# Key, query and tile-partial stores on the SyncE queue, first backward tiles pipelined, fewer warm-up matmuls

## The chip, the cores and the metric

One core of one Trainium2 chip. The metric is the device time of one execution in microseconds (us), lower is better. Where a time stands alone it is the median of the runs of one kernel on one chip.

## The reference

Forward and gradients of a block `x + s * g`. `g` is a gated MLP. `s` is attention over 64 segments of 32 tokens, each of which first sees 8 memory rows that the segment before it produced:

```python
H, Dh = (32, 128)               # 32 heads of 128; Dm = 640, S = 2048
M, seg = (8, 32)                # 8 memory rows, segments of 32 tokens
mem = mem0
for s in range(n_seg):          # 64 segments, one after another
    xs = x[:, s * seg_len:(s + 1) * seg_len, :]
    h = jnp.concatenate([mem, xs], axis=1)
    q, k, v = (einsum('btd,dhe->bhte', h, W) for W in (Wq, Wk, Wv))   # shortened
    scores = jnp.where(mask, einsum('bhqe,bhke->bhqk', q, k) * scale, -1e9)
    p = softmax(scores)
    o = einsum('bhte,hed->btd', einsum('bhqk,bhke->bhqe', p, v), Wo)
    mem = o[:, :M, :]
    outs.append(o[:, M:, :])
...
_out, _vjp = jax.vjp(_f, A_x, A_mem0, A_Wq, A_Wk, A_Wv, A_Wo, B_w1, B_w3, B_w2)
_grads = _vjp(grad_out)
```

The 64 memory updates are a serial chain, forward and again backward. The change touches those two chains and the start of the second.

## The kernel before

One forward step (`chain`) projects 32 columns with each weight: the 8 memory rows of this segment, and 24 *later* tokens that ride along. Keys, queries and values of these 32 rows are staged in a tile of 128 partitions by 1024 and stored. Three staging tiles a step share two buffers:

```python
WARM = dict(G1=1, G2=2, G3=3, G4=4, G5=3, G6=2)
...
def stage():
    return ch.tile([P, 1024], BF16, name="stg", tag="stg", bufs=2)

def dump(sg, dst, q=nc.gpsimd):
    q.dma_start(dst.rearrange("r (g c) -> g r c", g=4), sg[:])
sk = stage()
half(Wk_, 0, sk, 'v')
half(Wk_, 1, sk, 'v')
...
sq = stage()
...
dump(sk, k.KS[t])
...
sv = stage()                                # waits for the store of sk
packed_half(k, bA, hx, Wv, 0)
...
k.copy(sv[:, 0:512], bA[:], eng='s')        # line 92 of a helper, ACT
dump(sq, k.QVS[t, :, 0])
...
nc.scalar.copy(sTm[:], psT.rearrange("p a q h -> p a (q h)"))     # scores, ACT too
...
dump(sv, k.QVS[t, :, 1], nc.sync)
```

`gap("G2")` and the like, left out above, are places between the links of the chain into which other work is put (attention for the tokens, in tiles of 96), and then `WARM` matmuls whose result nobody reads; they keep TensorE's clock up:

```python
def gap(g):
    FILL(g, t, at, kbatch)
    ...
    for i in range(WARM.get(g, 0)):
        nc.tensor.matmul(bB[:], k.ident[:], Wq[:, 0, 0:512], start=True, stop=True)
```

Keys, queries and values of the first 672 tokens (`NB0`) were computed ahead and lie in order. Those of later tokens lie where the steps put them, in rows 8 to 32 of each step's block, so that 96 tokens are a block of 4 by 24 rows. The gradient rows (`g_src`) are likewise in order only from token 1344 (`GB0`) on:

```python
if x0 + nx <= self.NB0:
    return [(0, nx, X0[x0:x0 + nx])]                        # 96 rows in order
...
if r == 0 and nx - a >= 48:
    nt = (nx - a) // 24
    out.append((a, a + 24 * nt, XS[t:t + nt, 8:32]))        # 4 x 24 rows
...
def g_src(self, tl, c0, c1):
    ...
    return [(0, 96, self.GOS[8 + 4 * tl:12 + 4 * tl, 8:32, c0:c1])]   # 4 x 24 rows
```

The backward chain, cut to what the change touches:

```python
WARM = dict(G1=2, G2=3, G5=3, G6=2)
...
def load_xp(t):
    xp = ch.tile([P, 8, 2, 32], F32, name="xp", tag="xp", bufs=1)
    nc.sync.dma_start(xp[:], k.GXP[t // 3, :, :, t % 3])
...
sg = ch.tile([P, 1024], BF16, name="gstg", tag="gstg", bufs=1)
...
nc.sync.dma_start(k.GOS[t].rearrange("r (g c) -> g r c", g=4), sg[:])
...
def ld(tl, qd):                              # loads of a tile part, 4 ahead
    ...
    nc.sync.dma_start(qv[0:nm], k.m_src(tl, "qv", c0, c0 + 512))
    k.load_x(qv, nm, k.x_src(tl, "qv", c0, c0 + 512), nc.sync)
    k.load_x(gor, nm, k.g_src(tl, c0, c0 + 512), nc.sync)
    ...
def gmem(tl, qd):                            # tile partials, summed by gkv in a later step
    ...
    ks = fl.tile([P, ns, 2, 4, 8], F32, name="gks", tag="gks", bufs=1)
    ...
    nc.gpsimd.dma_start(k.GXP[tl, :, qd, 0:ns], ks[:].rearrange("p s i h m -> p s i (h m)"))
```

## Time and profile before

| | before |
|---|---|
| median of the runs before the prediction | 6971.42 us (3 runs, 6968.43 to 7006.38) |
| forward recurrence, 63 steps | 1613.1 us, 25.6 a step |
| start of the backward stage | 120.6 us |
| backward recurrence from its second step | 1482.0 us (2780.0 to 4262.0), 23.2 a step |

A step is the time from one step's first projection matmul to the next one's. The table can be checked against the page of the kernel before, of which these are the span and two rows of the slices (40 equal slices; granted clock in tenths of full, and busy share of the 16 DMA engines in tenths):

```profile
span 6956.7 us, 170429 instructions
...
PEclk9888888888888886888888997999999999885789
DMA  6473444444344554555555665233222233455673
```

The forward recurrence is slices 4 to 13, the backward one slices 16 to 25. The clock's digit is 8 in every slice of the first and 6 to 9 in the second; the means over the two stages are 0.87 and 0.88. The rest of the profile before is shown in the prediction.

### The profile page before, as it was taken

Reading aid. Unit: us, or ns where it says so; the run is one execution under the profiler, and the core shown is the slowest. Engines: PE = TensorE matmul, PEld = TensorE weight load, DVE = VectorE, ACT = ScalarE, POOL = GpSimd, SP = SyncE. Lnnn points to the kernel's source line nnn. Section 1 sums busy time; section 2 is a strip of 40 time slices with the busy share of each in tenths; the row PEclk is TensorE's granted clock in tenths of the full one; section 3 lists DMA queues with packets and bytes.
Section 4 is the critical chain, followed back from the end, with each engine's and each line's share of the span. In section 5 each row is a group of like instructions: output and inputs, shape, how many; then the busy total and the mean of one; then the engine's idle time right before and its main releaser. Section 6 shows DMA issues by size and latency. Waiting matters only on the chain. (4 is left out here: it accounts for less than half of the span.)

```text
span 6956.7 us, 170429 instructions
## 1 busy us (share of the span) xinstructions
PE 5767.0 (83%) x69516; PEld 3253.2 (47%) x69516; DVE 2419.9 (35%) x7541; ACT 1878.1 (27%) x5180; POOL 1184.8 (17%) x1811
## 2 busy tenths in 40 slices
PE   6777999898888775888888895988999988775688
PEld 3444444444444443555455553555555555342244
DVE  5433444444444212443334441222222222011752
ACT  3332444344334212222222221222222222000301
POOL 0001333333334102333333330000000000000000
PEclk9888888888888886888888997999999999885789
DMA  6473444444344554555555665233222233455673
GB/s 193 147 263 111 103 108 107 107 105 108 104 106 111 138 186 124 147 152 141 142 139 152 158 156 89 78 93 82 80 76 78 77 93 89 105 146 180 195 176 95
DMA packets 1039599, 876.70 MB, mean 126 GB/s; under 512 B 550536, under 2 KB 947304, under 8 KB 1029600
## 3 DMA queue, kind: packets, MB, share of 16 engines
q1 hardware_dynamic: 614330, 517.84, 27.3%
q10 hardware_dynamic: 337894, 213.14, 11.1%
q0 software_dynamic: 86592, 134.83, 7.9%
q8 instruction: 547, 8.96, 0.6%
q14 instruction: 236, 1.93, 0.1%
HBM read 556.09 MB, written 309.09 MB: 124 GB/s over the span
## 5 line engine op out<-in xcount | busy, mean ns | idle before, releaser
L1199 PE MATMUL g<-w,gT 128*128 128x512 bf16 x2112 | 622.7, 385 | 0.8 <-ACT gT L92 0.8
L1216 PE MATMUL wg<-gr,hr 120*128 120x512 bf16 (+1 forms) x2640 | 578.5, 379 | 1.0 <-DVE ghacc L1205 0.5
L1200 PE MATMUL g<-w,gT 128*128 128x128 bf16 x2112 | 466.9, 221 | 0.0
L662 PE MATMUL bank<-Wq,ident 128*128 128x512 bf16 x960 | 352.1, 474 | 138.1 <-ACT stg L92 138.1
L1216 PEld LDWEIGHTS <-hr 120*128 120x128 bf16 (+1 forms) x2640 | 254.0, 98 | 321.4 <-issue 22.6
L1199 PEld LDWEIGHTS <-gT 128*128 128x128 bf16 x2112 | 209.3, 99 | 220.9 <-issue 13.9
L1205 DVE TENSOR_TENSOR ghacc<-ghacc,g 120x512 f32<-120x512 f32 (+1 forms) x154 | 105.8, 687 | 563.4 <-PE g L1199 563.4
L1096 PE MATMUL gbank<-WqT,ident 128*128 128x512 bf16 x640 | 226.7, 461 | 83.6 <-DVE gkv L871 83.6
L1209 POOL CAST gxo<-ghacc 120x640 bf16<-120x640 f32 (+1 forms) x22 | 15.8, 720 | 1590.3 <-issue 1476.3
L92 ACT COPY gT<-t6g 128x480 bf16<-128x480 bf16 (+1 forms) x352 | 191.8, 545 | 331.1 <-PE t6g L1190 215.8
L337 PEld LDWEIGHTS <-gkv 128*8 128x8 bf16 x8192 | 201.7, 94 | 157.3 <-issue 49.8
L318 PEld LDWEIGHTS <-hx 128*32 128x32 bf16 x7680 | 178.0, 96 | 189.5 <-DVE xPT L624 25.5
L90 DVE CAST stg<-bank 128x512 bf16<-128x512 f32 x256 | 177.0, 691 | 235.9 <-PE bank L318 209.1
L604 ACT ACTIVATE xP<-xsp,xnm 120x120 bf16<-120x120 f32 (+1 forms) x704 | 239.7, 359 | 28.9 <-DVE xrz L614 18.2
L484 DVE COPY vt<-stg 8x512 bf16<-8x512 bf16 x512 | 144.5, 282 | 273.2 <-ACT stg L92 267.0
L90 DVE CAST wgo<-wg 128x512 bf16<-128x512 f32 x72 | 47.5, 688 | 543.6 <-PE wg L1216 499.0
L1241 PE MATMUL oa<-gow,orr 120*128 120x512 bf16 x704 | 197.2, 383 | 35.3 <-DMA orr<-OR 35.3
L1190 PE MATMUL t6g<-ident,gr 120*128 120x120 bf16 (+1 forms) x2112 | 187.9, 219 | 43.3 <-ACT gT L92 40.8
L983 POOL DMA_DIRECT2D VTD<-gvT x176 | 132.7, 789 | 462.9 <-ACT gvT L982 452.1
L1200 PEld LDWEIGHTS <-gT 128*128 128x128 bf16 x2112 | 209.0, 99 | 0.3
L615 POOL TENSOR_TENSOR xP<-xP,xrz 120x480 bf16<-120x480 bf16 (+1 forms) x176 | 170.3, 967 | 212.9 <-DVE xrz L614 202.9
L337 PE MATMUL gbank<-WvT,gkv 128*8 128x320 bf16 x4096 | 202.1, 366 | 0.0
(317 smaller groups left out, 11964.6 us busy)
## 6 DMA issues: line engine op xcount, KB each, us to landing
gqv<-QVS SPq DMA_DIRECT2D x112, 192.0 KB
vTt<-VTD SPq DMA_DIRECT2D x64, 320.0 KB
OR<-xv POOLq DMA_DIRECT2D x168, 120.0 KB, 4.6
VTD<-gvT POOLq DMA_DIRECT2D x168, 120.0 KB, 5.7
orr<-OR SPq DMA_DIRECT2D x8, 2520.0 KB
PR<-xP POOLq DMA_DIRECT2D x168, 112.5 KB, 7.0
gPr<-PR SPq DMA_DIRECT2D x168, 112.5 KB
DSR<-gdS POOLq DMA_DIRECT2D x168, 112.5 KB, 4.6
```

The lines of the kernel that those rows point to most:

```text
L90: return nc.vector.tensor_copy(out, in_)
L92: return nc.scalar.copy(out, in_)
L318: k.nc.tensor.matmul(bank[32 * g:32 * g + 32, :], x[:, dc, :], W[:, dc, c0:c0 + 512], start=(dc == 0), stop=(dc == k.DC - 1), tile_positio ...
L337: k.nc.tensor.matmul(pm[p0:p0 + nq, 0:320], x[:, h, :], W[:, h, 320 * b:320 * b + 320], start=(first and i == 0), stop=(last and i == 15), ...
L604: nc.scalar.activation(Pb[0:n, j, 0:n], sp[0:n, j, :], ACT.Exp, bias=nmx[0:n, j:j + 1], scale=k.scale, accum_out=Z[0:n, j:j + 1])
L662: nc.tensor.matmul(bB[:], k.ident[:], Wq[:, 0, 0:512], start=True, stop=True)
L1096: nc.tensor.matmul((bA if g[0] == "W" or g == "G1" else bB)[:], k.ident[:], WqT[:, 0, 0:512], start=True, stop=True)
L1190: nc.tensor.transpose(pt[:, j, :], gr[0:n, i, j * P:(j + 1) * P], k.ident[0:n, 0:n])
L1199: nc.tensor.matmul(g5[:], gT[:, i, j, :], W[:, j, 0:512], start=f, stop=l)
L1200: nc.tensor.matmul(g1[:], gT[:, i, j, :], W[:, j, 512:640], start=f, stop=l)
L1216: nc.tensor.matmul(accs[dc][:], hr[0:n, tl, dc * P:(dc + 1) * P], grs[tl][0:n, 2 - i, :], start=(tl == 0), stop=(tl == NTL - 1))
L1241: nc.tensor.matmul(ac[j][0][:], lh, gow[0:n, tl, 0:512], start=(tl == 0), stop=(tl == NTL - 1))
```

## The change

The intent: the value copy waits for the key store, so send that store earlier, from the SyncE queue; load the tile partials earlier; pipeline the 19 tile parts at the start of the backward stage; and drop warm-ups (15 to 7 a step forward, 10 to 4 backward), which should no longer be needed once the stalls are gone.

```diff
-            WARM = dict(G1=1, G2=2, G3=3, G4=4, G5=3, G6=2)
+            WARM = dict(G2=2, G3=1, G4=2, G5=2)
...
-                def dump(sg, dst, q=nc.gpsimd):
+                def dump(sg, dst, q=nc.sync):
...
-            WARM = dict(G1=2, G2=3, G5=3, G6=2)
+            WARM = dict(G1=1, G5=2, G6=1)
...
-                nc.gpsimd.dma_start(k.GXP[tl, :, qd, 0:ns], ks[:].rearrange("p s i h m -> p s i (h m)"))
+                nc.sync.dma_start(k.GXP[tl, :, qd, 0:ns], ks[:].rearrange("p s i h m -> p s i (h m)"))
...
-            for qd in range(8):
-                ld(k.NTL - 1, qd)
-                turn(k.NTL - 1, qd)
-                dprob(k.NTL - 1, qd)
-                dsoft(k.NTL - 1, qd)
-                gmem(k.NTL - 1, qd)
...
-            batch = {T - 1: [(k.NTL - 2, qd) for qd in range(8)] + parts[0]}
+            pro = [(tl, qd) for tl in (k.NTL - 1, k.NTL - 2) for qd in range(8)] + parts[0]
+            batch = {}
...
-                    if t == T - 1:          # (and the 11 parts that ran one after another in it)
...
                     elif g == "G4":
+                        if t > 0:
+                            load_xp(t - 1)
                         at(dsoft, t, 1)
...
                     elif g == "G6":
                         at(dsoft, t, 2)
-                        if t > 0:
-                            load_xp(t - 1)
...
+            todo = pro + todo
+            for _ in range(4):
+                ld_next()
+            for i in range(len(pro) + 2):
+                for f, o in ((turn, 0), (dprob, 1), (dsoft, 1), (gmem_ld, 2)):
+                    if 0 <= i - o < len(pro):
+                        f(*pro[i - o])
```

More of the change, by code (lines that the diff above doesn't have):

```diff
@@ L915, in chain @@
                 bd(nc.vector, bdS, dS)
-                if 0 < t < T - 1:
+                if t > 0:
                     loads(t - 1)
@@ L1061, in gap @@
                 def gap(g):
-                    if t == T - 1:
-                        if g == "G6":
-                            for u in batch[t]:
-                                ld_next()
-                                for f in (turn, dprob, dsoft, gmem):
-                                    f(*u)
-                            loads(t - 1)
-                            load_xp(t - 1)
-                            for _ in range(4):
-                                ld_next()
-                    elif g == "W0":
+                    if g == "W0":
                         at(turn, t, 0)
@@ L1075, in gap @@
                         at(turn, t, 1)
-                        if t + 1 < T - 1:
-                            at(gmem_ld, t + 1, 2)
+                        at(gmem_ld, t + 1, 2)
                     elif g == "G1":
@@ L1085, in gap @@
                     elif g == "G4":
+                        if t > 0:
+                            load_xp(t - 1)
                         at(dsoft, t, 1)
@@ L1092, in gap @@
                         at(dsoft, t, 2)
-                        if t > 0:
-                            load_xp(t - 1)
                     for i in range(WARM.get(g, 0)):
```

## The prediction

> **What bounds the kernel now.** I read the page's slices first, to see which stages the change touches and what clock they ran at; then the page's costliest groups, for the warm-up matmuls; then the waits of each engine, in the forward recurrence (611 to 2224 us of the span) and the backward one (2780 to 4242 us) separately; then the timeline of one step of each.
>
> The windows view of the forward recurrence, the start of the backward stage, and the rest of it:
>
> ```profile
> 610.90:2224.00 1613.10, 1445.58 (x22245) 767.10 (x22247) 701.51 (x2089) 626.70 (x2212) 585.30 (x787) 0.87 0.40 103
> 2659.40:2780.00 120.60, 57.31 (x782) 37.63 (x782) 37.44 (x249) 23.91 (x98) 35.42 (x62) 0.57 0.40 112
> 2780.00:4242.30 1462.30, 1247.01 (x24559) 772.28 (x24558) 590.42 (x2766) 376.52 (x1228) 484.74 (x840) 0.88 0.56 144
> ```
>
> The columns are length, busy PE, weight loads, DVE, ACT, POOL, then granted clock. The three stretches are 3196 of 6957 us; nothing else is touched. PE is busy 90% and 85% of the two recurrences, but not all of that is work. A forward step lasts 25.6 us, a backward one 23.2. The groups with the warm-up matmuls:
>
> ```profile
> L662 PE MATMUL bank<-Wq,ident 128*128 128x512 bf16 x960 | 352.1, 474 | 138.1 <-ACT stg L92 138.1
> L1096 PE MATMUL gbank<-WqT,ident 128*128 128x512 bf16 x640 | 226.7, 461 | 83.6 <-DVE gkv L871 83.6
> ```
>
> That is 15 warm-ups a step forward and 10 backward, and nearly the only real idleness of PE stands in front of them: 138.1/64 = 2.2 us a step forward, 83.6/64 = 1.3 us backward. Behind the first are ACT's waits in the forward stage:
>
> ```profile
> ACT stg L92 <- DMA KS<-stg: 306.3, 57, 12.4
> ACT stg L92 <- DMA OR<-xv: 28.9, 6, 5.6
> ```
>
> The staging tile has two buffers and three users a step (key, query, value), so the value copy waits until the key store has landed. One step's timeline, cut to this chain:
>
> ```profile
> 1406.20 0.76 POOL L456 DMA_DIRECT2D KS<-stg  x1
> ...
> 1413.80 1.07 ACT L92 CAST stg<-bank 128x512 bf16<-128x512 f32 x2 [5.23 <-DMA OR<-xv]
> ...
> 1414.93 0.58 PE L662 MATMUL bank<-Wq,ident 128*128 128x512 bf16 x1 [2.28 <-ACT stg L92]
> 1415.24 0.37 ACT L491 CAST sTm<-bank 40x256 bf16<-40x256 f32 x1
> ```
>
> The data for the value copy was ready at 1409.1; the copy began at 1413.8. ACT works in order, so the scores copy (L491), on which the recurrence hangs, is late too. The backward counterpart, in the waits of DVE, PE, ACT and POOL:
>
> ```profile
> DVE gkv L871 <- DMA xp<-GXP: 135.1, 28, 7.4
> PE gbank L1096 <- DVE gkv L871: 82.7, 62, 5.6
> PE gbank L326 <- ACT gstg L92: 49.0, 16, 5.6
> ACT gks L1027 <- DMA GXP<-gks: 164.4, 72, 9.0
> POOL gox L826 <- DMA gride<-GST: 78.9, 13, 8.4
> ```
>
> The load of the tile partials (xp) is issued at the end of a step and lands about 7.5 us later, after its user is ready. Every fourth step POOL waits for a token load; GXP stores queue behind that, ACT waits to reuse gks (one buffer), and the next step's gstg copy waits behind ACT.
>
> [...]the clock is half or full[...]: records are 0.5 or 1.0 and last multiples of 3.413 us. I summed the columns streamed in each window (512 columns at full clock are 0.21 us): in the forward stage the 63 windows after which the clock fell held 0.09 to 0.46 of a window's worth, and those after which it stayed full held at least 0.88; backward the two groups meet near 0.35. Each forward step falls once and stays cold 6.4 us on average.
> [...]Here the key store on GpSimd lands a median 7.0 us after issue; the value store, same shape, goes out on SyncE already and its last packet ends a median 7.4 us after issue. So the queue alone is not the gain. [...]This store is 4 by 32 by 1024; [...]about 23 of 2 KB in each half microsecond, 84 ns each, so four at a time, and 128 of them need 128 x 0.084 / 4 = 2.7 us at best.
>
> **The change part by part.**
> *Forward.* Mean marks of the 62 inner steps, from the first key matmul, us: value half ready 7.0; value copy 11.35; score matmuls end 9.6; scores transposed 13.1; softmax done 15.4; output product 17.6; Wo product 19.85 to 22.55; fold 23.65; next step 25.55. Now the key store goes out on SyncE as soon as the stage is filled, 3.2 us into the step (before: 4.1, behind an OR store). With 1.5 to 2 us to the first packet, 2.7 us of drain and about 1 us of sharing it should land near 9.0. Then the value copies end at 10.2, scores are transposed at 11.1 (-2.0), softmax is done at 13.2. Warm-ups in a row cost 0.22 us each at full clock (four in 1.04 us at 1395.71) and 0.42 at half (four in 1.89 us at 1421.78). Before the output product one is left of three, before Wo two of four: output product at 14.2, Wo at 15.8 to 18.2 (-4.0, half of it stall and half warm-ups and clock). The fold chain (ACT, DVE, ACT, DVE: 1.1 us) stays; dropping two warm-ups after it saves 0.3 us or so. Next step near 20.9: 4.6 us less. The stretch from 8.6 to 15.8 then holds 8048 columns, 3.35 us of 7.2, or 0.47: close to where the clock falls. I take off 0.6 us (40% of the steps cold, 1.5 us each): 4.0 x 63 = **252 us**.
> *Backward.* Steps without the xp stall and without a cold window exist: steps 24, 22, 17, 12 and 8 take 19.3 to 19.9 us with all ten warm-ups; in them the first output product starts at 8.0 us, in stalled ones at 11 to 15. The load now goes out in mid-step, right after its buffer's last reader, ahead of the tile loads; that is over 8 us earlier. GXP stores on SyncE no longer stand behind POOL's token wait. Three warm-ups between gkv and the product go, 3 x 0.22 = 0.65; the other three hide mostly behind the fold, 0.2. So 19.7 - 0.85 = 18.9, plus 0.9 for cold windows in most steps (unstalled steps with one take 20 to 21): 19.8 against 23.2, 3.4 x 62 = **211 us**.
> *Start.* From the first load (2659.4) to the second step (2780.0) are 120.6 us at clock 0.57: 8 tile parts in 37 us, then a first step of 83.8 that holds 11 more, one after another. Pipelined, 19 parts are limited by SyncE's issues, 2.6 to 2.9 us each plus 0.55 for the store, say 3.4: 65, plus 12 to fill and drain, plus a step of 21: 98. **22 us**.
> Sum 252 + 211 + 22 = 485; 6971 - 485 = 6486, so 6485.
>
> **The rivals.**
> *The store is no faster on SyncE.* For it: the 7.4 us of the value store. Against: that one has ten or so loads ahead of it in its ring, the key store two to four. The value copy would start at 10.6 instead of 9.0, costing 1.6 us a step, 100 us: 6585.
> *Fewer warm-ups, colder clock.* For it: 0.47 is near the 0.46 at which the clock has fallen. If both chains ran cold from scores to product in each step, forward would lose about 1 us more a step and backward as much: 125 us, 6610. Against: the stalls that caused the falls are what goes.
> *SyncE in order becomes the bound.* Its issues already take 15 to 20 us of a 25 us step in the middle of the backward stage, and gain 1.5; forward the loads now stand behind two stores that wait for data. If middle backward steps stick at 22 us, 90 us are lost: 6575. Against: SyncE waits 4.2 us a step for the krow buffer, and tile loads run four ahead.
> Two together give about 6700; all three about 6800, still over 2% less. To come within 2% (above 6832) the stalls must stay whole.
>
> **Range and chances.** One rival wholly or two in half give 6575 to 6630; everything going right (no cold windows) is near 6390. So 6390 to 6630, with faster 0.94, same 0.05, slower 0.01.
>
> **What would show it.** Right: forward step near 21.5 us and backward near 20; ACT's wait for the key store below 100 us in all (now 306); DVE's wait for xp gone; gstg waits under 15 us; clock above 0.92 in both stretches; start stretch near 98 us. Wrong: ACT still waiting for KS over 3 us a step (first rival); clock at or below 0.87 with short PE gaps (second); waits of PE or DVE for DMA loads of gqv, xq, xv or xp (third).

## The result

| | before | changed | predicted |
|---|---|---|---|
| median, same chip, 4 runs each | 6969.93 us | 6864.44 us | 6485 (6390 to 6630) |
| ratio (95% interval) | 1 | 0.984 (0.9805 to 0.9874) | about 0.93 |
| forward step, mean of all | 25.60 us | 24.69 us | 21.5 |
| of these steps 1 to 17 / 19 to 59 | 25.56 / 25.55 | **22.18 / 25.79** | no difference expected |
| backward step | 23.23 us | 22.46 us | 19.8 |
| start of the backward stage | 120.6 us | 126.0 us | 98 |

A ratio is the mean time of one kernel's runs over that of the other kernel's runs of the same rounds, so it is not quite the ratio of the medians quoted. The experiments ran on chips 7, 12 and 6; the times of the kernel before differ between chips by up to 0.4%, so they are compared with each other by ratio. Step times are from the profiled execution of each.

About 105 us were gained instead of 485. By stages of the two profiles: forward 1613.1 to 1555.6 (-57.5), backward 1482.0 to 1438.2 (-43.8), start +5.4. The sum, -95.9, is the difference of the spans, 6956.7 to 6863.8, within 3 us; nothing was lost elsewhere.

The windows view of the changed kernel, the same three stretches (length, busy PE, weight loads, DVE, ACT, POOL, granted clock, DMA share, GB/s):

```profile
612.30:2167.90 1555.60, 1305.35 (x21610) 730.35 (x21735) 709.10 (x2089) 625.15 (x2211) 487.92 (x659) 0.87 0.40 107
2603.10:2729.10 126.00, 46.02 (x774) 35.02 (x776) 37.42 (x250) 25.60 (x100) 24.66 (x43) 0.55 0.44 117
2729.10:4167.30 1438.20, 1166.57 (x24054) 769.96 (x24180) 589.81 (x2766) 381.38 (x1226) 396.74 (x683) 0.87 0.58 146
```

PE is busy 140 and 80 us less than before in the two recurrences, because the warm-ups are gone, but the stretches shrank by only 57 and 44: PE idles more. The clock is where it was. What PE waits for, in the waits of ACT and PE in the forward stretch (idle us, count, longest):

```profile
ACT stg L92 <- DMA KS<-stg: 309.7, 57, 8.7
PE bank L497 <- ACT sTm L491: 163.4, 63, 5.2
```

The wait of the value copy for the key store, 306.3 us before, is 309.7. It was to fall below 100. But it is not spread evenly. The timeline of step 14, cut to the issue of the key store, the value copy and the first matmul that needs the scores:

```profile
930.72 0.55 SPq L456 DMA_DIRECT2D KS<-stg  x1
...
936.59 1.07 ACT L92 CAST stg<-bank 128x512 bf16<-128x512 f32 x2 [2.47 <-PE xpo L632]
...
938.46 0.22 PE L497 MATMUL bank<-ident,sTm 40*128 40x40 bf16 x2 [0.46 <-ACT sTm L491]
```

and the same three of step 36:

```profile
1478.21 0.68 SPq L456 DMA_DIRECT2D KS<-stg  x1
...
1488.45 1.07 ACT L92 CAST stg<-bank 128x512 bf16<-128x512 f32 x2 [7.87 <-DMA KS<-stg]
...
1489.83 0.24 PE L497 MATMUL bank<-ident,sTm 40*128 40x40 bf16 x2 [4.49 <-ACT sTm L491]
```

The bracket is the idle time just before, and what ended it. In step 14 the copy follows the issue of the store by 5.9 us and waits for no DMA; in step 36 by 10.2 us, of which ACT stands still 7.9. The store was issued 3.1 us into step 14 and 3.9 us into step 36, near the 3.2 predicted. What differs is the loads beside it: the key tiles come from the 4 by 24 blocks from step 18 on, the query and value tiles from steps 23 and 24. SyncE also issues two DMAs a step more from then on (18.5 for 16.5), but the store's own issue is no later for it, 3.2 us into the step on average.

The DMA view of step 36, from the issue of the key store to 1488 (the first row has 40 slices of 0.25 us, the busy share of the 16 engines in tenths; below it some of the issues of this stretch):

```profile
DMA  3225645413000128652223242222222222222222
...
KS<-stg SPq DMA_DIRECT2D x1, 256.0 KB
...
xq<-QVS SPq DMA_DIRECT2D x2, 96.0 KB
```

The store's first packet came 5.4 us after the issue, after slice 22. Loads that were issued before it pass first (in slices 11 to 13 the engines are nearly idle; what the loads wait for there, the trace does not tell). From slice 19 on, two tenths of the 16 engines are busy, seldom more: about four of sixteen. The store is 4 by 32 rows and the loads around it are 4 by 24.

The packets in the trace say where the time goes, if the 2 KB packets (84 ns each) are given to the stores in the order of their issue. In steps 1 to 17 the key store's first packet came 1.3 us after the issue on average (1.2 at best, 0.65 after the issue's end) and its last 4.5 us after the first; in steps 19 to 59, 3.8 us and 3.9 us. So the drain is no slower in late steps. The wait before it is longer, and in that wait 3.5 packets of the SyncE queue are in flight on average. The loads' 1 KB packets (46 ns each) are in flight 3.8 at a time in late steps and 8.0 in early ones (means over the packets).

The trace does not name the engines that a packet ran on, but it can be counted whether loads and stores add up. In steps 19 to 59, 1 KB packets of loads and 2 KB packets of stores are in flight together for 17% of the time, 2.0 and 1.9 of them on average. Together that is 3.9, and it is more than five in only 4% of that time. In steps 1 to 17, with most loads in order, the same sum is 6.0; in e4 below, where the stores spread wider, it is 8.4. Apart, the loads of late steps are in flight 3.8 at a time and the 2 KB packets 3.5 (means over the packets): on two separate sets of engines some seven should be in flight together, on one shared set about four. So the counts speak for the same four engines; that is an estimate from these counts.

Backward, the waits of DVE, ACT and PE in the changed kernel:

```profile
DVE gkv L871 <- ACT gOst L900: 227.4, 63, 7.4
ACT gks L1027 <- DMA GXP<-gks: 206.2, 61, 7.3
PE gvpt L979 <- DMA gqv<-QVS: 56.0, 23, 3.7
PE gbank L326 <- ACT gstg L92: 48.8, 31, 3.9
PE ggpt L986 <- DMA gor<-GOS: 19.4, 23, 2.1
```

DVE's wait for the tile partials (xp, 135.1 us before) is gone, as predicted. In its place PE waits for the tile loads (gqv and gor, 75 us; before, together 1.5 us), and the waits for the store of gks and behind gstg have not shrunk. DVE's 227 us behind ACT's gOst copy are no new stall: that copy starts 0.07 us after the transposes that it reads. In the start stretch PE stands 46.9 us for gqv loads.

### The profile page after: what moved, and what is told of

Its sections match the earlier page's. It is cut to its first block, busy times and chain, and to the rows that moved or that the text cites. A ratio compares the mean times of both kernels' runs of the same rounds, so it can differ in the third digit from the quotient of the medians.

```text
span 6863.8 us, 167869 instructions
## 1 busy us (share of the span) xinstructions
PE 5507.1 (80%) x68068; PEld 3209.3 (47%) x68620; DVE 2423.3 (35%) x7541; ACT 1884.3 (27%) x5180; POOL 987.8 (14%) x1507
## 5 line engine op out<-in xcount | busy, mean ns | idle before, releaser
L1190 PE MATMUL g<-w,gT 128*128 128x512 bf16 x1936 | 573.0, 384 | 0.7 <-ACT gT L92 0.7
L337 PE MATMUL gbank<-WvT,gkv 128*8 128x320 bf16 x4096 | 238.6, 413 | 26.6 <-DVE gkv L871 26.6
L337 PE MATMUL bank<-Wo,oTm 128*8 128x320 bf16 x4032 | 209.2, 379 | 1.3
L1465 PE MATMUL w2acc<-gzB_all,hb_tok 128*128 128x128 bf16 (+3 forms) x437 | 122.8, 434 | 87.8 <-DMA hb_tok<-HB 82.7
```

What stands on the lines that cost most here:

```text
L337: k.nc.tensor.matmul(pm[p0:p0 + nq, 0:320], x[:, h, :], W[:, h, 320 * b:320 * b + 320], start=(first and i == 0), stop=(last and i == 15), ...
L1190: nc.tensor.matmul(g5[:], gT[:, i, j, :], W[:, j, 0:512], start=f, stop=l)
L1465: nc.tensor.matmul(accs[ci][0:fsz, 0:dsz], hb[:, fc * P:fc * P + fsz], gzB_all[:, tt, d0:d0 + dsz], start=(tt == 0), stop=(tt == NT - 1))
```

## The experiments

The theories. **F (fan-out)**, the main one: the 4-wide stores now queue behind 4-wide loads and share a few DMA engines with them (3.9 packets in flight together, above), so the key store lands as late as ever in steps past the 18th, and the tile loads of the backward stage land late behind the stores. **Issue order**: SyncE, whose issues stand one after another in the timeline, is what is full, and stores that wait for data (forward, 186.3 us for DVE's stg copies) hold the loads behind them. **C (clock)**: with the warm-ups gone the clock falls and eats the gain. In the short diffs, `+` is the experiment; e1 to e7, e9, e11 and e12 start from the changed kernel, e8, e10 and e13 from the kernel before (there is no e5). Ratios are against the kernel before.

### e1: key and query stores back on GpSimd

```diff
-                def dump(sg, dst, q=nc.sync):
+                def dump(sg, dst, q=nc.gpsimd):
```

> The changed kernel with only the key and query stores back on the GpSimd queue. Theory F (few DMA engines: in the SyncE ring a store of 4 by 32 rows and, from forward step 19 on, the loads of 4 by 24 rows are drained by about four engines at a time, so the ring is full in 96% of the late forward time and the store lands 7.5 to 9 us after issue): the first 18 forward steps lose about 2 us each (mean 22.3 to about 24.3) and the later ones gain about 1 (25.6 to about 24.6), total 6850 to 6870 against 6864. Rival R (SyncE issues the store late, in order): same loss early, no gain late, 6890 or more. Rival C (the missing gain is the colder clock of fewer warm-ups alone): every forward step gets slower by 1 to 2 us, 6930 or more.

Measured: 6851.58 us (before 6943.16), ratio 0.9867 (0.985 to 0.9883). Forward steps 1 to 17 took 24.50 us (22.18 in the changed kernel), steps 19 to 59 took 25.14 (25.79). So the SyncE queue is worth 2.3 us a step as long as the loads are in order. Beside 4-wide loads nothing clear is left of it: it loses 0.65 us here and gains 0.30 in e10, and e3, whose forward stage is the changed kernel's own, took 25.47 us there, 0.32 less than the changed kernel. That the total lies in the expected range is partly luck, since this chip is 0.4% faster: 0.9867 of 6970 would be 6877.

### e2: the old warm-ups in the changed kernel

```diff
-            WARM = dict(G2=2, G3=1, G4=2, G5=2)
+            WARM = dict(G1=1, G2=2, G3=3, G4=4, G5=3, G6=2)
-            WARM = dict(G1=1, G5=2, G6=1)
+            WARM = dict(G1=2, G2=3, G5=3, G6=2)
```

> The changed kernel with the old warm-up counts (15 forward, 10 backward). Theory F: the clock is second order; forward steps grow by about 1.2 us (8 matmuls, half of them behind waits), backward ones stay within 0.5 us of 22.4, cold time falls in both; total 6900 to 6960. Rival C: backward steps lose their one cold window each and fall to about 21.7 and forward cold time falls from 395 us to under 300; total 6800 to 6864.

Measured: 6853.9 us (before 6943.16), ratio 0.9874 (0.9857 to 0.989). The expectation was missed, and not only because this chip is faster: 0.9874 of 6970 would be 6882. Forward steps grew by 0.1 us (24.69 to 24.80), not by 1.2. By ratio the warm-ups cost 0.34%, some 24 us, but the interval overlaps that of the changed kernel, so no difference is shown. They do what they are for: the cold time (at half clock) falls from 395 to 303 us forward and from 368 to 322 backward. The time does not fall with it. Clock is not what the gain was lost to.

### e3: tile-partial stores back on GpSimd

```diff
-                nc.sync.dma_start(k.GXP[tl, :, qd, 0:ns], ...
+                nc.gpsimd.dma_start(k.GXP[tl, :, qd, 0:ns], ...
```

> The changed kernel with the tile partials stored from the GpSimd queue again (their load stays early). Theory F: backward SyncE is the late one (PE waits 56 us for gqv and 19 us for gor loads that before it did not wait for), and taking 176 stores of 0.36 us and their waits for ACT (68.5 us) off it gives 30 to 80 us back: 6785 to 6835; the waits of PE for gqv and gor fall below 35 us. Rival (the backward loads are late because of the four-engine loads in the ring, whoever issues the store): within 15 us of 6864, or slower by up to 50 because the stall behind the every-fourth-step token load on GpSimd comes back.

Measured: 6807.56 us (before 6943.16), ratio 0.9796 (0.9774 to 0.9818). This part of the change seems to have lost 0.44%, about 31 us, though the intervals still overlap (up to 0.9818 here, from 0.9805 there): the start is back to 117.7 us from 126.0, PE's wait for gqv falls from 61 to 33 us over the whole backward stretch, and a backward step from 22.46 to 22.19. The waits for gks (223 us) and behind gstg (53.4) stay, so GpSimd's place in the queue was not their only cause.

### e4: the same stores on the same queue, each cut into four

```diff
-                    q.dma_start(dst.rearrange("r (g c) -> g r c", g=4), sg[:])
+                    for g_ in range(4):
+                        q.dma_start(dst[:, g_ * 1024:(g_ + 1) * 1024], sg[32 * g_:32 * g_ + 32, :])
```

> The changed kernel with each key, query and value store cut into four DMAs of 32 rows, so that each can spread over more DMA engines; all on SyncE, nine more issues a step. Theory F: the key store lands within about 4 us of its issue, ACT's wait for it falls from 310 us below 120, late forward steps go from 25.6 to about 23.3, early ones by 0.5 to 1; total 6740 to 6790. Rival R (SyncE's issue order and time is what is short): nine issues of about 0.5 us make it worse, late forward steps above 26, total above 6880.

Each store is now four DMAs whose outermost dimension is 32 rows. The bytes and the queue are the same, SyncE issues 9 more DMAs a step. Measured: 6603.28 us (before 6943.16), ratio **0.9505** (0.949 to 0.9521). The windows view, forward and backward:

```profile
609.40:1923.90 1314.50, 1216.76 (x21740) 697.68 (x21741) 709.34 (x2089) 635.94 (x2211) 489.91 (x659) 0.96 0.48 127
2477.60:3915.80 1438.20, 1186.59 (x24180) 771.12 (x24180) 590.22 (x2766) 381.13 (x1226) 396.79 (x683) 0.87 0.58 146
```

The forward stretch fell by 241 us, at clock 0.96 with the few warm-ups; the backward one, whose stores this edit does not touch, is the same to the tenth. ACT's waits forward, a late step of the timeline, and the DMA row of that step's first 5 us (40 slices of 0.13 us):

```profile
ACT stg L92 <- DMA KS<-stg: 71.1, 33, 6.7
```

```profile
1481.93 1.73 SPq L457 DMA_DIRECT2D KS<-stg  x4
...
1486.32 0.59 ACT L92 CAST stg<-bank 128x512 bf16<-128x512 f32 x1 [1.20 <-DMA KS<-stg]
```

```profile
DMA  2222225974695989496878411100006922697195
```

The copy follows the first issue by 4.4 us, with the same 4-wide loads around. The row begins with two tenths, while earlier work drains four at a time, and then goes to six to nine: the store now uses the other engines too. The late forward steps take 21.1 us (25.8 in the changed kernel). The gain is larger than expected (23.3 us, total 6740 to 6790). "Issue order" cannot explain this, since SyncE issues more than before.

### e6: loads in order instead, the 4-wide stores left alone

```diff
-        self.NB0 = 672
+        self.NB0 = 2048
-        self.GB0 = 1344
+        self.GB0 = 0
```

(and the loops that compute those rows ahead, 16 blocks of 128 tokens for 6 of 112)

> The changed kernel with all token rows of key, query, value and output gradient computed ahead, so that every tile load reads 96 rows in one piece instead of 4 by 24 (same number of DMAs, same bytes; the stores stay narrow). The extra work ahead of both recurrences costs some 300 us, so steps are compared, not totals. Theory F (loads of 4 by 24 rows keep about four DMA engines busy[...]): late forward steps fall from 25.8 us to the early ones' 22.2, mid backward steps (24 to 41) from 23.9 to about 20.9 as in the last 21 steps, PE's wait for gqv and gor (61 and 20 us) to under 15, and the start of the backward stage from 126 us to under 100. Rival R (SyncE's number of issues is what is short): steps and start within 0.5 us, or 5 us for the start, of the changed kernel's.

This is the other side of the collision. It computes far more ahead, so its total (6898.93 us, one look) says nothing; its steps do. They also lack the 24 riding tokens' loads and copies forward, for which only GpSimd was seen to wait (46 us), and SyncE issues about one DMA a step less (17.3 for 18.5 in late forward steps, 23.5 for 24.5 in middle backward ones), so the expectation's "same number of DMAs" is not quite met. Windows, forward and backward, and ACT's wait in the forward stretch:

```profile
866.20:2298.90 1432.70, 1262.40 (x21610) 709.64 (x21735) 708.97 (x2089) 622.64 (x2210) 471.02 (x603) 0.92 0.46 115
2916.60:4212.20 1295.60, 1130.20 (x24054) 751.01 (x24180) 589.08 (x2766) 378.24 (x1226) 396.92 (x683) 0.91 0.65 162
```

```profile
ACT stg L92 <- DMA KS<-stg: 208.8, 59, 10.5
```

Waits of PE in the backward stretch:

```profile
PE gvpt L979 <- DMA gqv<-QVX: 4.2, 5, 1.6
PE ggpt L986 <- DMA gor<-GX: 4.1, 7, 1.0
PE gbank L326 <- ACT gstg L92: 4.8, 9, 1.6
```

Forward steps 22.63 early and 22.78 late: the difference between early and late is gone with the 4-wide loads. The first packet of the key store comes 1.2 us after the issue in both. The narrow store itself is still waited for (208.8 us; 71.1 in e4). Backward steps 20.20 us, close to the 19.8 predicted for the changed kernel; start 104.8, not under the 100 expected here. The three waits above were 56.0, 19.4 and 48.8 us. So the backward mechanism of the prediction was there; it needed loads that land in time.

### e7: e4, and the gradient store cut the same way

```diff
-                nc.sync.dma_start(k.GOS[t].rearrange("r (g c) -> g r c", g=4), sg[:])
+                for g_ in range(4):
+                    nc.sync.dma_start(k.GOS[t][:, g_ * 1024:(g_ + 1) * 1024], sg[32 * g_:32 * g_ + 32, :])
```

> The kernel with wide stores of the round before (e4), and the backward step's GOS store cut into four DMAs as well. Theory F: the GOS store takes 2.7 us of four engines each step; freed, mid backward steps fall from 24.2 by 0.5 to 1.5 us, 20 to 60 us in all, to about 6550 to 6585 on a chip where e4 takes 6603. Rival R: three more issues in SyncE's already full order cost 20 to 60 us.

Measured: 6527.54 us (before 6960.85), ratio **0.9384** (0.9365 to 0.9404), the fastest version tried and faster than both kernels. The backward step falls from 22.56 (e4) to 21.25 us; 1.31 x 62 = 81 us, and the ratio fell by 1.2%, 84 us. That is more than the 20 to 60 us expected, with three more issues a step. Gstg stalls fall from 46.7 to 16.4 us. The start is still 124.3.

### e8 and e10: the kernel before with only the stores on SyncE, cut (e8) or not (e10)

```diff
-                def dump(sg, dst, q=nc.gpsimd):
+                def dump(sg, dst, q=nc.sync):
```

(e8 also has the edit of e4)

> The kernel before with one change: its key, query and value stores go out on SyncE, cut into four DMAs each; warm-ups, backward stage and all else as before. Theory F: the stall on the staging buffer goes and the forward step falls from 25.6 to about 21.8 us (e4 had 20.9 with 8 fewer warm-ups), total about 6970 - 240 = 6730, ratio 0.965 to 0.970. Rival C (it is the warm-ups that e4 needed gone): forward step above 23.5, ratio above 0.98.

> The kernel before with its key and query stores moved to SyncE in one piece each, as the change does, and nothing else. Theory F: the first 18 forward steps gain about 2.5 us each, the later ones nothing or lose up to 0.5, so 20 to 45 us in all, ratio 0.993 to 0.998, where the same stores in four pieces gave 0.958. If the narrow store costs nothing: ratio near 0.96.

Measured: e8 6668.64 us (before 6960.85), ratio 0.9584 (0.9566 to 0.9601); e10 6900.27 (before 6961.34), ratio 0.991 (0.9881 to 0.9938). With nothing else of the change and all old warm-ups, the queue alone is worth 0.9% and queue and cut together 4.2%. Forward steps early/late: e10 22.37/25.25, e8 21.04/21.36. The forward windows of e8 and ACT's wait in e10:

```profile
609.70:1950.30 1340.60, 1289.78 (x22115) 720.61 (x22241) 709.80 (x2089) 637.43 (x2212) 488.89 (x660) 0.98 0.47 124
```

```profile
ACT stg L92 <- DMA KS<-stg: 259.4, 54, 10.5
```

### e9 and e13: the warm-ups, on top of e4 and on the kernel before

e9 is e4 with the old warm-ups (the edit of e2); e13 is the kernel before with the new ones (its reverse).

> e4 (wide stores) with the old warm-up counts. If the dropped warm-ups are worth what the prediction said once the stall is gone (about 1.2 us a forward step, 0.8 us a backward step): slower than e4 by 100 to 130 us. If the colder clock takes it back: within 30 us of e4.

> The kernel before with the new warm-up counts alone. While the stalls are still there, the warm-ups stand mostly in or just behind them and keep the clock up: gain of 0 to 50 us (ratio 0.993 to 1.0), cold time above the 411 and 359 us of before. If the prediction's 0.2 to 0.4 us a warm-up were right whatever the stall: 120 us or more, ratio below 0.983.

Measured: e9 6642.11 us (before 6960.85), ratio 0.9551 (0.953 to 0.9571), which makes the dropped warm-ups worth 0.46%, about 32 us, to e4. e13 6878.51 (before 6961.34), ratio 0.9875 (0.9845 to 0.9905): 1.25%. Each result lies between the two cases of its expectation (100 to 130 us or within 30; above 0.993 or below 0.983), so neither case was right. In e13 the key store is as late as before, and the saved matmuls show at once (forward step 25.60 to 24.86, backward 23.23 to 22.89) although the clock is colder (cold time 426 and 413 us, 411 and 359 before). In e9 forward steps run almost without cold time (39 us), and a warm-up at full clock is cheap (0.22 us in a row, 0.42 at half clock, in the trace before) and partly hidden. The worth of a part depends on what else is there; the parts do not add up.

### e11 and e12: e7 with the partial stores on GpSimd, then with the backward loads cut too

```diff
+        if getattr(self, 'split', False):          # on in the backward stage only
+            return [(24 * i, 24 * i + 24, self.GOS[8 + 4 * tl + i, 8:32, c0:c1]) for i in range(4)]
         return [(0, 96, self.GOS[8 + 4 * tl:12 + 4 * tl, 8:32, c0:c1])]
```

(e11 is e7 with the edit of e3; e12 is e11 with the lines above, and the same for gqv in `tok_src`)

> e7 (wide key, query, value and GOS stores) with the tile partials stored from the GpSimd queue again. On the changed kernel this was worth 0.4% by the ratios. Theory F, with a ring now less full: 15 to 40 us less than e7, ratio 0.933 to 0.936. Rival (with free DMA engines SyncE's store is the quicker one, and GpSimd's every-fourth-step wait for a token load delays it): 0.938 or more. This is the candidate for a version better than both kernels.

> e11 with the backward tile loads of 4 by 24 rows cut into four loads of 24 rows each (about 16 more issues of 0.35 us a step on SyncE[...]). Theory F alone: mid backward steps fall from about 22 to near 20.5, ratio 0.925 to 0.930. Rival R (issue time on SyncE, now short): SyncE is busy 15 us of a 22 us step already, so 5.6 us more make it the bound, mid steps above 23, ratio above 0.938.

Measured: e11 6541.35 us, ratio 0.9398 (0.937 to 0.9426), no different from e7; the 15 to 40 us expected did not come. PE's wait for gqv falls from 31 to 5 us, but the wait behind gstg returns (16.4 to 50.9 us), as ACT again waits longer for the stores of gks (140 to 187 us). e12: 6651.18 us, ratio 0.9552 (0.9528 to 0.9576), 1.6% slower than e11. PE's waits in the backward stretch of e12:

```profile
PE gvpt L983 <- DMA gqv<-QVS: 82.8, 17, 8.0
...
PE gbank L320 <- POOL gox L829: 41.2, 8, 7.9
```

Sixteen more issues a step put SyncE's issue time from 0.65 to 0.88 of the middle backward steps, and the loads are late for that reason now. So the rival "issue order" is real, at this dose, and cutting is not free: with 9 more issues a step in e4 it paid, with 16 more in the fuller backward stage it did not.

Not tried: a third staging buffer, which would remove the wait itself, does not fit in memory beside the rest of the forward stage: the build stops, with 5.5 KB a partition left for tiles that take 7.25.

## Why the prediction was wrong

**The step that failed** is the key store's landing: "With 1.5 to 2 us to the first packet, 2.7 us of drain and about 1 us of sharing it should land near 9.0." The issue at 3.2 us was right (3.1 to 3.2 on average). The drain with its sharing, 3.7 us together, was near what was measured (4.5 us in steps 1 to 17, 3.9 in steps 19 to 59). The term that was mis-sized is the first, the author's estimate (in the trace before, the first 2 KB packet of the SyncE queue came 1.2 to 3.4 us after the issue of the value store, median 2.2): the first packet came 1.3 us after the issue in early steps, but 3.8 us after it (1.3 to 6.0) in late ones, where the store stands behind 4-wide loads in the same queue. So the value copy, forecast from 9.0 us on, began at 9.35 us in early steps and at 12.3 in late ones, and the step took 22.2 and 25.8 us instead of 21.5. Of the 252 us, 57 came. The 4.3 us by which 42 or so late steps exceed 21.5 make 180 of the 195 us that are missing. That the step could be had is shown by e4: 20.9 us mean.

The prediction counted "two to four" loads ahead of the key store, and step 36 has three of 96 rows. It did not ask how wide they are: at four packets at a time, 96 x 46 ns / 4 = 1.1 us each (an estimate from the packets). It had looked at one step (1406 us). Its 2 KB packets, four at a time, were those of the value store; on GpSimd the key store went out in packets of 4 KB.

**Rival 1** (the store no faster on SyncE) is thus what happened in two thirds of the steps, with a different reason from the one given there: not the number of DMAs ahead in the ring, but their shape. It was priced at 100 us, with the value copy at 10.6 us and 1.6 us lost a step; the copy came at 12.3 and 4.3 us were lost.

**The clock** (rival 2) was predicted above 0.92 and stayed at 0.87. But as the cause it is refuted: giving back the warm-ups (e2) cuts the cold time and gains nothing, and taking the store's delay away (e4) brings 0.96 forward with the same few warm-ups. Forward, the cold windows followed the stalls. The level of 0.46 that made the prediction take off 0.6 us a step does not hold either: counted in the same way, windows of 3.413 us in the changed kernel's forward stage that held 0.31 kept the clock, and some that held up to 1.26 lost it (in the kernel before, backward: from 0.32 kept, up to 0.40 lost).

**Backward**, the removal of the xp stall was right (135.1 to 0), the end of the gstg stalls was not (49.0 to 48.8), and the step came to 22.46 instead of 19.8: 44 us for 211. The term missing is the third rival, waits for gqv and gor (75 us), and with them the wait behind gstg that stayed (49 us); that is 124 of the 165 us missing, and the rest is not assigned. The step of the estimate that failed is its sample. The five steps taken as a model (24, 22, 17, 12 and 8) lie where query and value tiles already load in order, which in that trace begins in step 26. Steps 24 to 1 took 21.51 us before and 21.12 changed; steps 47 to 25, where both kinds of load are 4 wide, 25.05 and 24.22; in e6 the two groups take 20.03 and 20.28. That narrow transfers are behind it is shown by the store (e7: 21.25 us with three more issues a step) and supported by the loads (e6: 20.20 us, one look). What was said for SyncE's order as the bound, its share of issue time, holds only in part: e3 suggests that taking the partial stores off it gives some 31 us back, and e12 that a fuller SyncE does become the bound.

**The start** grew by 5.4 us instead of shrinking by 22. Pipelining was to leave SyncE's issues as the limit; PE waited 46.9 us for gqv instead. In e6 it took 104.8 us, and with the partial stores on GpSimd (e3) 117.7, against 120.6 before; so pipelining gained little where the loads stayed as they were.

**The warm-ups** were not listed apart in the sum. In the kernel before they are worth 1.25% (e13), in the changed one 0.34% (e2 against it, within the intervals). With 0.9% for the queue (e10), the product of e10 and e13 is 0.9786; the changed kernel without its partial stores on SyncE (e3) is 0.9796. Within their intervals the moved xp load and the pipelined start add nothing that can be seen.

What stays open: how much of the start's wait is narrow loads and how much SyncE's issue; and the 41 us backward that no wait named here accounts for. That the four engines are the same four rests on counts of packets, not on their names.

## What to carry to other kernels

Before a store is moved to another queue, write down for it *and for every transfer in that queue at that time* the size of the outermost dimension; here 4-wide transfers in the SyncE queue shared about a quarter of the engines, which the DMA row of the profile shows as a steady two tenths. Cutting such a store into pieces with 32 rows outermost gave 3.4% here for nine more issues a step, while the move itself gave 0.9% in the kernel before and nothing clear (0.3%) in the changed one; look at the issuing engine's load before cutting more. And read a step early and one late in a loop, and ask of a step taken as a model whether its loads have the shape of the others': the same code ran 3.6 us apart because its loads changed shape on the way.
